# Loading the first kernel tile through two queues, and negating its second half on VectorE

## The chip, the cores and the metric

The kernel runs on one core of a Trainium2 chip. Its time is the device time of one execution in microseconds (us). Each version is executed several times and the median is compared. One execution is also profiled; its trace gives the start, the length and the releaser of each instruction on TensorE (PE, with its weight loads PEld), VectorE (DVE), ScalarE (ACT), GpSimd (POOL) and the DMA queue of SyncE (SP). Trace times are counted from the start of the profiled span.

## The reference

The program computes two independent things and joins their outputs. Part A is a recurrent attention over 64 segments; the change doesn't touch it, but it fills the second two thirds of the time. Part B is a long convolution by way of a transform:

```python
P = jnp.exp(logdA[:, :, None] * l[None, None, :])      # l = 0 .. 2047
K = jnp.einsum('dn,dnl,dn->dl', Cc, P, dB).real        # one kernel per channel d
Kf = rfft2(pad(K))                                     # spectrum of the kernel
Uf = rfft2(pad(u transposed))                          # spectrum of the input
y = irfft2(Uf * Kf)[..., :L] transposed + u * Dskip
```

There are D = 1024 channels, N = 128 states and L = 2048 positions; all inputs are bf16.

## The kernel before

Part B comes first and part A follows. Part B is written in an order set by hand: each engine and each queue carries out its instructions in the order in which the program names them.

**Tables.** The kernel K is built from tables of exponentials and sines, 64 channels at a time, in 16 passes. The loop `for f in range(-1, 17)` (line 1116) walks the words of the list ORDER (line 600). A word names an operation and a slot; a prime means that the word belongs to the pass before (r = f - 1), so the passes overlap. The last iteration, f = 16, has only the primed words of pass 15 left to do. The words that matter here:

- `b0'`, `b1'`: `absolute`, line 1068, an absolute value in place on `nr` (VectorE, 128x1856, four bytes an element).
- `w0'`, `w1'`: `minus`, line 1075, `wn`, minus the sine (VectorE, 128x768 bf16).
- `C0'`, `C1'`: `cosine`, line 1071 (ScalarE), after `absolute`.
- `gi`, `gr`: `products`, lines 1019 and 1020 (VectorE), from the sine or cosine and the exponentials.
- `K0'` to `K3'`: `part`, line 910, small matmuls into `kp` (TensorE), and `x0'` to `x3'`: `part_out`, line 918, which casts `kp` into `KxT` (VectorE).
- After pass 3, 7, 11 and 15 `KxT` holds 256 channels and is written to `Kd` in DRAM by a set of small DMAs (line 925), taken one by one from the list `late`. What is left at the end goes to SP and GpSimd in turn.

**Side work.** Between these words other work is done in small portions: `U` (the input's spectrum, line 866, with sums `us` on VectorE, lines 877 and 878, sums `ux` on GpSimd, lines 882 to 885, and a write to `Ud`, line 886), `M` (transposed matrices, `ms`, line 849, written to `MId` by GpSimd, line 850), and `P` (projections that part A will need, lines 145 and 158, with writes `PVd` and `PKd` on SP).

**The first kernel tile.** At f = 15 the first 512 channels of K have long been in DRAM. `load_k` (line 946) fetches them as one tile `KT` of 128x16x512 bf16 with 31 DMAs (line 954), from rows that are interleaved for the transform. Its argument `qs` is a tuple of queues that take the DMAs in turn; here it holds SP alone. `negate` (line 987) makes `KN`, minus the second half of `KT` (128x4096), with one tensor_scalar: before, on GpSimd (line 990), at the word `m'` of f = 15. In GpSimd's queue it stands behind the Ud write of the previous portion and ahead of the MId write and the ux sums of its own.

**The spectrum of the kernel.** `spectrum(0)` (line 1007), first thing of f = 16, is 64 matmuls on TensorE into the PSUM tiles `pa` and `ptt`; 16 of them read KN. From then on a loop over b = 0 to 15 makes `spectrum(b + 1)`, multiplies with the input's spectrum on VectorE (`pointwise`, lines 1182 to 1193, input `uq` by line 981 on SP), and from b = 4 transforms back (`inverses`, line 1240, with `uu` loaded and written by GpSimd). The later channels of K are loaded at b = 0 by 62 DMAs on GpSimd (line 954 too).

Of the kernel before, what the change touches and what calls it, by code (L numbers as in the profile page):

```python
# [10 lines left out]
BF16 = mybir.dt.bfloat16  # L11
# [595 lines left out]
def part_b(ctx, tc, u, A_re, A_im, B_re, B_im, C_re, C_im, log_dt, Dskip, out_b, ahead, copies, residents, first_state):  # L607
# [5 lines left out]
    DH, DQ = 512, 256  # L613
    v, sc, gp, pe, sy = nc.vector, nc.scalar, nc.gpsimd, nc.tensor, nc.sync
# [331 lines left out]
    def load_k(d0, n_d, qs, KT):  # L946
        dsl = slice(d0, d0 + n_d)

        def rows(r0, n, step=1):
            return Kd[r0:r0 + step * (n - 1) + 1:step, dsl]  # L950
        n_q = [0]

        def get(out, in_):
            qs[n_q[0] % len(qs)].dma_start(out=out, in_=in_)
            n_q[0] += 1
        for r in (0, 2, 1, 3):
            k0 = KT[:, 4 * r, :]
            get(k0[0:64], rows(r, 64, 4))
            get(k0[64:128], rows(256 + (0, 0, 1, 2)[r], 64, 2))
            k1 = KT[:, 4 * r + 1, :]  # L960
            if r == 2:
                get(k1[0:128:2], rows(384, 64, 2))
                get(k1[1:128:2], rows(386, 64, 2))
            else:
                get(k1[:], rows(384 + (0, 0, 0, 1)[r], 128))
            for mc in (2, 3):
                k2 = KT[:, 4 * r + mc, :]
                q0 = 512 + 64 * (mc - 2)
                get(k2[0:128:2], rows(q0, 64))
                if r == 0:  # L970
                    get(k2[1:128:4], rows(q0, 32, 2))
                    get(k2[3:128:4], rows(q0 + 2, 32, 2))
                else:
                    get(k2[1:128:2], rows(q0 + 1, 64))
        return KT

    def load_u(b):
        us = []
        for n_ in range(2):
            t_ = ahead.pool.tile([128, 2, 2, DQ], F32, name="uq", tag="wsl", bufs=4)  # L980
            sy.dma_start(out=t_[:].rearrange("p a c d -> p (a c d)"), in_=Ud[b % 4, b // 4][:, 2 * n_:2 * n_ + 2].rearrange("p a c d -> p (a c d)"))
            us.append(t_)
        return us
# [3 lines left out]
    def negate(KT, eng=None):  # L987
        KN = ahead.pool.tile([128, 8, DH], BF16, name="KN", tag="xTl")
        if eng:
            eng.tensor_scalar(out=KN[:], in0=KT[:, 8:16, :], scalar1=-1.0, scalar2=None, op0=ALU.mult)  # L990
        else:
            for i in range(2):
                sc.activation(out=KN[:, :, DQ * i:DQ * i + DQ], in_=KT[i][:, 8:16, :], func=ACT.Copy, scale=-1.0)
        KNs.append(KN)

    def spectrum(b, s_):
        dq, kc = b // 4, b % 4
        KN = KNs[dq // 2]
        d = slice(DQ * (dq % 2), DQ * (dq % 2) + DQ)
        KT = ks[0][:, :, d] if dq < 2 else ks[dq - 1][:]  # L1000
        for half in range(2):
            for r in range(2):
                for cs in range(2):
                    for i, rr in enumerate((r, r + 2)):
                        for mc in range(4):
                            rhs = KN[:, 4 * (rr - 2) + mc, d] if half == 1 and i == 1 else KT[:, 4 * rr + mc, :]
                            pe.matmul(s_[r][half][:, cs, :], lhsT=MF[:, kc, 4 * rr + mc, cs, :], rhs=rhs,  # L1007
                                      start=(i == 0 and mc == 0), stop=(i == 1 and mc == 3), skip_group_check=True)
# [83 lines left out]
    def run_side(kind, slot):  # L1092
        for g in side_ops[kind]:
            f_ = next(g, g)
            if f_ is not g:
                pending[kind, slot] = f_
                return

    def run_evict(kind, slot, copy):
        f_ = pending.pop((kind, slot), None)  # L1100
        if f_ is not None and f_.__code__.co_argcount:
            f_(copy)
        elif f_ is not None:
            f_()
# [11 lines left out]
    for f in range(-1, 17):  # L1116
        if f == 15:
            for kind, slot in sorted(k for k in pending if k[0] == "P"):
                run_evict(kind, slot, v.tensor_copy)
            while ahead.late:  # L1120
                ahead.late.pop(0)()
            ks = [load_k(0, DH, (sy,), ahead.pool.tile([128, 16, DH], BF16, name="KT", tag="kst"))]
        if f == 16:
            spectra = [load_u(0), load_u(1)]
        for word in ORDER:
            nm, r = word.rstrip("'"), f - word.endswith("'")
            if f == 15 and word == "m'":
                negate(ks[0], gp)
            if f == 16 and word == ORDER[0]:
                s0 = ps_e.tile([128, 2, 512], F32, name="pa", tag="pa")  # L1130
                s1 = [ps_t.tile([128, 512], F32, name="ptt", tag="ptt") for _ in range(2)]
                first = [[s0[:, half, :].rearrange("p (c d) -> p c d", c=2) for half in range(2)],
                         [t_[:].rearrange("p (c d) -> p c d", c=2) for t_ in s1]]
                spectrum(0, first)
            if nm in evict_of:
                run_evict(*evict_of[nm])
            elif nm[0] in side_ops:
                if f >= 0:
                    run_side(nm[0], int(nm[1:] or 0))
            elif nm[0] == "X":  # L1140
                e = int(nm[1])
                if 0 <= r <= 15 - (e == 0) or (r == -1 and e == 0):
                    table_ops[nm[2]](r, e)
            elif 0 <= r <= 15:
                table_ops[nm[:-1]](r, int(nm[-1]))
# [171 lines left out]
def kernel(  # L1317
# [88 lines left out]
    with ExitStack() as ctx_b:  # L1406
        part_b(ctx_b, tc, B_u[0], B_A_re, B_A_im, B_B_re, B_B_im, B_C_re, B_C_im, B_log_dt, B_Dskip, out_b, ahead, copies, residents, first_state)
# [37 lines left out]
```

## Time and profile before

| what | value |
|---|---|
| median of 4 executions | 2399.77 us (2392.59 to 2406.52) |
| profiled execution | 2392.59 us |
| its span | 2390.9 us |
| busy: PE / PEld | 2002.3 / 1179.9 us |
| busy: DVE / ACT / POOL | 1481.6 / 976.9 / 362.1 us |
| mean granted TensorE clock | 0.966 |

The tables end at about 487 us, the loop over b runs to about 700 us, part A fills the rest. The stretch around the end of the tables, by the view of busy time per window:

| window, us | PE busy | DVE busy | POOL busy | granted clock | DMA share |
|---|---|---|---|---|---|
| 436 to 444 | 6.09 | 8.00 | 7.66 | 1.00 | 0.36 |
| 456 to 462 | 5.83 | 4.16 | 2.77 | 1.00 | 0.40 |
| 462 to 477 | 8.10 | 15.00 | 14.68 | 0.77 | 0.46 |
| 477 to 484 | 1.07 | 6.73 | 2.26 | 0.59 | 0.40 |
| 484 to 490 | 5.48 | 3.52 | 2.27 | 0.50 | 0.14 |
| 490 to 540 | 36.73 | 48.87 | 34.22 | 0.88 | 0.87 |
| 540 to 600 | 60.00 | 56.47 | 25.50 | 1.00 | 0.53 |

The granted clock is the share of full speed that TensorE was given; the DMA share is the mean busy share of the core's 16 DMA engines. In a timeline line the columns are the start, the length, the engine, the line of the program, the operation, output<-input, and in brackets the idle time before it with what ended it. "SPq" is the issue of a DMA by SyncE.

### The profile page before, as it was taken

The page shows a single profiled execution, that of the slowest core. Times are in us where ns is not written, and L with a number is a line of the kernel's source. Part 1 is how long each engine was busy: PE and PEld are TensorE (multiplying, and loading weights), DVE is VectorE, ACT ScalarE, POOL GpSimd, SP SyncE. Part 2 cuts the span into 40 slices and gives each one's busy share as a digit, 9 for nine tenths or more (in the row PEclk, how much of TensorE's full clock was granted, in tenths as well). Part 3 has the DMA queues.
Part 4 walks back from the last instruction along what each step waited for, and adds up shares of the span by engine and source line. Part 5 has one row for each costly group of instructions (what it writes and reads, how often), then busy time and mean ns, then how long its engine had stood idle before and what let it go on. Part 6 is the DMA issues. An engine that isn't in the chain of part 4 may idle for free.

```text
span 2390.9 us, 78400 instructions
## 1 busy us (share of the span) xinstructions
PE 2002.3 (84%) x33773; PEld 1179.9 (49%) x33798; DVE 1481.6 (62%) x3159; ACT 976.9 (41%) x1599; POOL 362.1 (15%) x609
## 2 busy tenths in 40 slices
PE   1699999769997888888888888888888888888889
PEld 1366665558883444444444444444444444444444
DVE  9599999999973555545455454554545545454540
ACT  6699999713342323323232232323323233332321
POOL 2245354564121000000000000000000000000020
PEclk6799999889998999999999999999999999999999
DMA  6786985575479999999999999999999999999992
GB/s 160 185 242 201 246 224 147 168 235 183 139 265 377 384 376 388 375 371 385 368 387 384 369 374 374 380 365 372 380 385 373 372 380 384 385 384 388 386 384 74
DMA packets 380384, 759.08 MB, mean 317 GB/s; under 512 B 121704, under 2 KB 213960, under 8 KB 377988
## 3 DMA queue, kind: packets, MB, share of 16 engines
q1 hardware_dynamic: 365316, 710.87, 82.6%
q0 software_dynamic: 14720, 43.20, 5.4%
q8 instruction: 264, 4.33, 0.7%
q14 instruction: 84, 0.69, 0.1%
HBM read 699.16 MB, written 67.88 MB: 321 GB/s over the span
## 4 chain that ended last, share of the span: by engine, by line
DMA 35%; PE 32%; DVE 15%; issue 8%; ACT 6%; SPq 1%; POOL 1%; ACTq 0%; DVEq 0%; POOLq 0%
DMA wst<-WD_k 14%; PE acc L349 14%; DMA wst<-WD_o 12%; PE pp L448 3%; DMA wst<-WD_v 3%; DVE nr L1068 2%; PE pe L571 2%; PE pro L158 2%; PE tr L360 2%; DMA out_dram<-uu 2%; PE ups L866 2%; DMA wst<-WD_q 2%; PE pa L1037 2%; DVE piece L282 1%; DMA KT<-Kd 1%
## 5 line engine op out<-in xcount | busy, mean ns | idle before, releaser
L349 PEld LDWEIGHTS <-hT 128*32 128x32 bf16 x12352 | 326.9, 97 | 454.5 <-issue 230.7
L349 PE MATMUL acc<-wst,hT 128*32 128x512 bf16 x3072 | 312.8, 391 | 145.7 <-DMA wst<-WD_q 51.0
L349 PE MATMUL acc<-W,hT 128*32 128x512 bf16 x5120 | 400.9, 384 | 0.0
L355 ACT CAST ev<-acc 128x512 bf16<-128x512 f32 x384 | 225.1, 586 | 399.6 <-PE acc L349 394.6
L448 PEld LDWEIGHTS <-oT 128*32 128x32 bf16 x8192 | 204.1, 97 | 122.6 <-issue 96.4
L282 DVE TENSOR_SCALAR piece<-keep 128x256 int32<-128x256 int32 (+1 forms) x640 | 192.4, 363 | 60.2 <-PE pp L448 31.9
L387 DVE TENSOR_REDUCE mx<-sc 128x8 f32<-128x320 f32 x128 | 62.4, 487 | 232.4 <-PE sc L380 232.3
L448 PE MATMUL pp<-W_o,oT 128*32 128x256 bf16 x4096 | 184.0, 277 | 5.5 <-DMA W_o<-in_A_Wo_dram 5.3
L361 DVE COPY KT<-tr 128x512 bf16<-128x512 bf16 x64 | 27.2, 425 | 259.4 <-PE tr L360 259.4
L448 PE MATMUL pp<-wst,oT 128*32 128x256 bf16 x2560 | 129.0, 278 | 43.2 <-DMA wst<-WD_o 34.0
L349 PE MATMUL acc<-MF,hT 128*32 128x512 bf16 x2048 | 158.5, 383 | 0.0
L368 POOL COPY KT<-pk 128x128 bf16<-128x128 bf16 x128 | 37.9, 296 | 783.5 <-PE sc L380 433.6
L361 ACT COPY QT<-tr 128x512 bf16<-128x512 bf16 x128 | 75.0, 586 | 178.7 <-PE tr L360 177.8
L435 ACT CAST oT<-pv 128x512 bf16<-128x512 f32 x128 | 75.1, 586 | 171.7 <-PE pv L421 170.1
L321 POOL COPY hT<-xt 128x192 bf16<-128x192 bf16 x63 | 22.0, 350 | 737.3 <-DMA xt<-XTd 446.5
L1007 PEld LDWEIGHTS <-MF 128*128 128x128 bf16 x1024 | 103.7, 102 | 36.0 <-issue 15.7
L158 PE MATMUL pro<-xTl,wsl 128*128 128x512 bf16 x493 | 116.3, 381 | 6.0 <-ACT xTl L102 5.2
L389 ACT ACTIVATE sc<-sc 128x320 f32<-128x320 f32 x128 | 54.0, 422 | 153.9 <-DVE sc L388 145.6
L360 PEld LDWEIGHTS <-ev 128*128 128x128 bf16 x1024 | 58.2, 98 | 97.3 <-issue 66.7
L1007 PE MATMUL hps<-KT,MF 128*128 128x256 bf16 x720 | 94.0, 283 | 13.8 <-DVE x L1183 10.7
L1240 PE MATMUL yp<-Bt,MI 128*128 128x256 bf16 x680 | 102.8, 273 | 0.8 <-ACT yb L1256 0.8
L360 PE MATMUL tr<-a_ident,ev 128*128 128x128 bf16 x1024 | 102.2, 223 | 0.0
(315 smaller groups left out, 3808.1 us busy)
## 6 DMA issues: line engine op xcount, KB each, us to landing
wst<-WD_o SPq DMA_DIRECT2D x320, 512.0 KB
wst<-WD_k SPq DMA_DIRECT2D x256, 512.0 KB
wst<-WD_q SPq DMA_DIRECT2D x256, 512.0 KB
wst<-WD_v SPq DMA_DIRECT2D x256, 512.0 KB
Ud<-ux POOLq DMA_DIRECT2D x16, 1024.0 KB, 5.7
uq<-Ud SPq DMA_DIRECT2D x32, 512.0 KB
pk<-PKd SPq DMA_DIRECT2D x64, 192.0 KB
wsl<-in_A_Wk_dram SPq DMA_DIRECT2D x16, 512.0 KB
```

The source lines that it names most:

```text
L158: nc.tensor.matmul(a[:], lhsT=w[:, kc, 128 * j:128 * j + 128], rhs=xTl[:, kc, :, :].rearrange("p s k -> p (s k)"), start=(kc == 0), stop=( ...
L282: nc.vector.tensor_scalar(out=out.bitcast(I32), in0=in_.bitcast(I32), scalar1=0, scalar2=None, op0=ALU.bitwise_or)
L349: nc.tensor.matmul(a[32 * g:32 * g + 32, o_:o_ + rhs.shape[1]], lhsT=hT[:, kc, :], rhs=rhs, start=(kc == 0), stop=(kc == KC - 1), tile_pos ...
L355: nc.scalar.copy(out=q[:], in_=a[:])
L360: nc.tensor.transpose(out=p[:, i, hl, :, :].rearrange("p a b -> p (a b)"), in_=q[:, 128 * hl:128 * hl + 128], identity=ident[:])
L361: eng(out=dst, in_=p[:, i, :, :, :])
L387: nc.vector.tensor_reduce(out=mx[:], in_=sc, axis=AX.X, op=ALU.max)
L389: nc.scalar.activation(out=sc, in_=sc, func=ACT.Exp, scale=scale)
L435: nc.scalar.copy(out=o[:], in_=p[:].rearrange("p a (g q) -> p a g q", g=4))
L448: nc.tensor.matmul(po[32 * qt:32 * qt + 32, :], lhsT=oT[:, h % 4, (h % 16) // 4, :], rhs=columns(w, 1024 * hh + 256 * qt, 256)[0][1], star ...
L1007: pe.matmul(s_[r][half][:, cs, :], lhsT=MF[:, kc, 4 * rr + mc, cs, :], rhs=rhs, start=(i == 0 and mc == 0), stop=(i == 1 and mc == 3), ski ...
L1240: pe.matmul(yp[:, b, :], lhsT=m_[:, b, cs, kc, :], rhs=Bt[:, kc, j, half, c_, :], start=(kc == 0 and cs == 0 and half == 0), stop=(kc == 3 ...
```

## The change

`KT` is loaded by SP and GpSimd in turn: DMAs 1, 3, 5 and so on go to SP (16), DMAs 2, 4, 6 and so on to GpSimd (15). `negate` moves from GpSimd, at the word `m'` of f = 15, to VectorE, at the start of f = 16, directly before `spectrum(0)` is issued. In VectorE's queue that places it behind the last cast `KxT` of `x3'` (f = 15) and ahead of `b0'` of f = 16. The data and their layout stay the same.

```diff
-            ks = [load_k(0, DH, (sy,), ahead.pool.tile([128, 16, DH], BF16, name="KT", tag="kst"))]
+            ks = [load_k(0, DH, (sy, gp), ahead.pool.tile([128, 16, DH], BF16, name="KT", tag="kst"))]
         if f == 16:
             spectra = [load_u(0), load_u(1)]
         for word in ORDER:
             nm, r = word.rstrip("'"), f - word.endswith("'")
-            if f == 15 and word == "m'":
-                negate(ks[0], gp)
             if f == 16 and word == ORDER[0]:
                 s0 = ps_e.tile([128, 2, 512], F32, name="pa", tag="pa")
                 s1 = [ps_t.tile([128, 512], F32, name="ptt", tag="ptt") for _ in range(2)]
                 first = [[s0[:, half, :].rearrange("p (c d) -> p c d", c=2) for half in range(2)],
                          [t_[:].rearrange("p (c d) -> p c d", c=2) for t_ in s1]]
+                negate(ks[0], v)
                 spectrum(0, first)
```

## The prediction

> **What bounds the kernel now.** I read the chain that ended last first, in order of time, because the change touches some 40 us of a 2390.9 us span and only a place on the chain can pay. Columns: start, length, what.
>
> ```profile
> 462.27 8.51 DVE nr L1068
> 470.79 5.58 DVE wn L1075
> 483.79 3.19 PE kp L910 x73
> 497.69 5.05 DMA PKd<-PVd
> 502.93 4.91 POOL KT L954 x9
> ```
>
> Two VectorE instructions of the last table pass are the longest pieces of this stretch, and the path then runs through kp, the Kd writes, the PKd copies and GpSimd's later KT loads into the pointwise phase. Next I read the timeline of VectorE, one table pass earlier and in the last pass (start us, length, what):
>
> ```profile
> 438.64 1.58 DVE L1068 TENSOR_SCALAR nr<-nr 128x1856 int32<-128x1856 int32 x1
> 440.15 0.88 DVE L1075 TENSOR_SCALAR wn<-sn 128x768 bf16<-128x768 bf16 x1
> 440.95 1.65 DVE L1068 TENSOR_SCALAR nr<-nr 128x1856 int32<-128x1856 int32 x1
> ...
> 462.24 8.54 DVE L1068 TENSOR_SCALAR nr<-nr 128x1856 int32<-128x1856 int32 x1
> 470.71 5.66 DVE L1075 TENSOR_SCALAR wn<-sn 128x768 bf16<-128x768 bf16 x1
> 476.29 1.12 DVE L1068 TENSOR_SCALAR nr<-nr 128x1856 int32<-128x1856 int32 x1
> 477.32 1.11 DVE L1019 TENSOR_TENSOR gi<-E,sn 128x1824 bf16<-128x1824 bf16 x1
> ```
>
> The same three instructions take 3.88 us from start to start of the next work in one pass (438.64 to 442.52, where the next row begins) and 15.08 us in the other (462.24 to 477.32). Their shapes are equal. GpSimd's timeline says what differs:
>
> ```profile
> 421.03 2.23 POOL L896 DMA_DIRECT2D pt<-PB  x4
> ...
> 438.52 4.67 POOL L885 TENSOR_TENSOR ux<-us 128x256 f32<-128x256 f32 x4
> 443.48 0.57 POOL L886 DMA_DIRECT2D Ud<-ux  x1 [0.30 <-POOL ux L885]
> 459.24 10.57 POOL L990 TENSOR_SCALAR KN<-KT 128x4096 bf16<-128x4096 bf16 x1 [15.18 <-DMA PVd<-vst]
> 469.77 1.13 POOL L850 DMA_DIRECT2D MId<-ms  x1
> 470.93 1.28 POOL L882 TENSOR_TENSOR ux<-us 128x512 f32<-128x512 f32 x1
> 472.16 1.27 POOL L883 TENSOR_TENSOR ux<-us 128x512 f32<-128x512 f32 x1
> 473.38 2.76 POOL L885 TENSOR_TENSOR ux<-us 128x256 f32<-128x256 f32 x4
> ```
>
> KN runs on GpSimd until 469.81, and L1068, begun at 462.24, ends at 470.78: about its own 1.12 us after KN. The wn behind it, 0.34 us when alone (the shortest of its 32), ends at 476.37, 0.23 us after the last ux. So these VectorE forms do not run while GpSimd works on SBUF. The negation on GpSimd costs VectorE its own length, and it also pushes ux (ready at 459.56, as the us row before it ends then) onto wn.
>
> SP's timeline carries the loads:
>
> ```profile
> 435.94 21.25 SPq L954 DMA_DIRECT2D KT<-Kd  x31
> ```
>
> **The change, part by part.** VectorE is on the path all the way from 462.24 to 477.32: no idle stands before any of these rows. I rebuild this stretch.
>
> *GpSimd loses KN, gains 15 load issues.* They stand where the table pass begins, behind the Ud write, so they start at 444.05 (443.48 + 0.57). The first of them waits for old Kd writes and for the kst tile's last DMA (issued 429.62), all past. Nearest rows: L896, four in 2.23 us, 0.56 each, at this same phase of an earlier pass; L954 itself, later, fifteen from 502.93 to 511.25, 0.55 each with landing waits. So 15 x 0.55 = 8.3 us, done at 452.4; landing, by KT's own DMAs, 3.3 to 7.2 us: 455.7 to 459.6. They are gone from the queue before MId, whose ms comes at 458.0. So MId and ux go back to their usual phase: ux's first row at 459.65, its L885 rows from 462.13, as in the pass before (first ux 436.05, L885 438.52).
>
> *The rule that speaks against this part* is in the Trainium skill, SBUF — State Buffer, section SBUF: two separate sides: descriptors of a DMA issued from GpSimd cannot be written while VectorE is in a two-port mode, and an issue of some 620 ns then took 3100. At that price the 15 issues take 46.5 us, end at 490.6, land at 495.8. The trace has rows for issues beside VectorE's work in this phase, 0.56, and the slowest Ud issue, in the last pass, is 1.08. In 444 to 452 VectorE runs products with two inputs, conversions, and only one wn (448.95, 0.36 us). I take the row: the rule costs 0.4 us here, hidden by 2.6 us or more of slack, if only wn can hold an issue up.
>
> *SP loses 15 of 31 issues.* At 21.25/31 = 0.69 each, SP is through at about 447 instead of 457.2. What follows (PVd, Kd, uq) moves earlier, but the next thing that matters on SP, the Kd writes of the last table, waits for KxT at 487 in any case. Worth nothing by itself.
>
> *VectorE gains KN*, queued behind the last KxT of the pass and ahead of L1068. It waits for KT's second half, landed by 459.6, so it can start at 462.24; queued behind it are both L1068, wn, and all products of the last pass. Length: no such row. Fitting fixed + per-element time to 1.116 us for 1856 four-byte elements and 0.343 for 768 two-byte ones at half the time each gives 0.141 us + n x 0.263 ns for bf16: 4096 elements take 1.22 us. Ends: below, 1.2; above, at L1068's time per element, 2.29. I take 1.22, since wn has the same operation and type.
>
> *Contention left.* ux's four L885 rows run from 462.13. In the pass before, each VectorE row waited for one of them (1.58, 0.88, 1.65 instead of 1.12, 0.34, 1.12). Now KN takes the first wait: KN 0.5 + 1.15 = 1.65, then 1.51, 0.80 and 1.57 (start to start in the pass before) make 5.5 us. **Saved: 15.08 - 5.5 = 9.5 us.**
>
> *A second rule to weigh*: the same page, section Who interferes with whom, says whoever issues first holds the shared pair for one whole instruction. By it KN loses at most one L885, 0.69 us. The row at 470.71 disagrees: wn waited through six GpSimd instructions. If KN does as wn did, it waits 2.76 us, but nothing is left for the others to wait for: 2.76 + 1.15 + 1.04 + 0.27 + 1.04 = 6.3, saved 8.8. Without any contention 3.5, saved 11.6. I take 9.5, the pattern of the pass before, because the phase is the same.
>
> *TensorE* waits 5.43 us for KN at 464.4 now. After: KN is ready at about 463.9. Its 32 remaining matmuls, at the 0.11 us of the first 16, end at 468, before gr (470.9). The 5.43 us are not added: they lay beside VectorE's stall. What is late next: VectorE's products, then kp. ACT's two cosines follow L1068 by 1.84 us and come before their products.
>
> *Does the shift reach the end?* After KxT come Kd writes, PKd copies, KT loads (502.93) and pointwise steps. All are behind KxT in their queues, so they move together. From 540 to 660 TensorE is busy 60.0 of each 60 us at clock 1.00 and DMA at 0.53 and 0.43: fixed work, its start moves. From 700 on the weights' stream holds DMA at 0.96; its slots come free as the phase ends, so it moves too.
>
> **The sum.** Profiled execution 2392.59 (span 2390.9) - 9.5 = 2383.1. It was the fastest of four; the same 9.5 off the median 2399.77 gives **2390**, which I forecast.
>
> **Rivals.**
>
> *More is gained.* No contention (11.6), and TensorE stays warm for kp: the clock is 0.59 and 0.50 in 477 to 490, where kp holds VectorE up for 2.0 us. Three quarters of kp took 1.7 us at 435, all of it 3.2 us here; at the faster pace (1.7 x 4/3 = 2.3) about 0.9 us go. Together 12.5: 2387. Against: TensorE still idles before gi ends, and each pass shows the contention.
>
> *Nothing arrives.* The gain ends in a wait on the DMAs that does not move, such as uu at 550, for which VectorE waits 2.08 us behind GpSimd's KT loads. Then 2400. Against: these loads are themselves behind KxT.
>
> *Slower: the loads on GpSimd land late.* KN is at the head of VectorE's queue, and everything waits for it. The gain is gone once the last load lands after 462.24 + 9.5 = 471.7: with 5.2 us of landing, when an issue takes over (471.7 - 5.2 - 444.05)/15 = 1.5 us. At the slowest row, 1.08, landing is at 465.5 and 6.2 us of gain are left. At the rule's 3.1 us, KN starts 33.6 us late: 24 us slower, 2424.
>
> *The change not doing what it says* is out: queue order has KN on VectorE and 15 loads on GpSimd.
>
> **How the numbers follow.** Forecast 0.60, more 0.25, nothing 0.08, slower 0.07. A measurement of this kernel tells about 0.5% from no change, 12 us. The forecast lies below that; the four runs spread over 14 us, so a third of its cases may measure above it, and about two thirds of the richer case: 0.19 + 0.16 = 0.35 faster. Slower: 0.06 from its rival, 0.02 from noise. Same: the rest, 0.57. The range: the four runs, less 9.5, are 2383 to 2397; unknown costs (8.4 with the long KN, 12.5 in the richer case) widen it down to 2380, noise of a median on another day and the case of no gain up to 2401; I take 2379 to 2401. The slower case is left out.
>
> **What would show it.** KN on VectorE at about 462.3, 1.2 to 1.8 us; L1068 and wn of the last pass at some 1.6 and 0.9; 15 KT issues of 0.55 on GpSimd from 444; no idle before TensorE's KN matmuls; the first pointwise row (L1182, now 488.22) near 478.7, and the uu wait and the end moved as much. It is wrong if KN waits for DMA past 464, if ux runs elsewhere than at 459.6 to 466, or if L1182 moves and the end does not.

## The result and the profile after

The changed kernel takes 2388.07 us (median of 40 executions, 2378.34 to 2399.77) against 2399.71 us (61 executions, 2390.62 to 2413.08) for the kernel before. The ratio of the mean times is 0.9956 with a 95% interval of 0.9946 to 0.9965: 10.6 us less, between 8.4 and 13 (the two medians lie 11.6 us apart). The profiled execution took 2383.52 us with a span of 2381.8, 9.1 us less than the span before. Its mean granted clock is 0.981, where the profile before has 0.966; the difference lies mostly ahead of the place of the change (0.93 before, 1.00 now, up to 440 us), and at the end of it VectorE comes to the stretch in question only 0.76 us earlier. Below line 1127 the changed program has one line less, so line 1182 of before is line 1181 here.

VectorE's timeline, around the end of the tables, in the changed kernel:

```profile
461.48 1.73 DVE L990 TENSOR_SCALAR KN<-KT 128x4096 bf16<-128x4096 bf16 x1
463.13 1.64 DVE L1068 TENSOR_SCALAR nr<-nr 128x1856 int32<-128x1856 int32 x1
464.70 0.88 DVE L1075 TENSOR_SCALAR wn<-sn 128x768 bf16<-128x768 bf16 x1
465.50 1.65 DVE L1068 TENSOR_SCALAR nr<-nr 128x1856 int32<-128x1856 int32 x1
467.08 1.11 DVE L1019 TENSOR_TENSOR gi<-E,sn 128x1824 bf16<-128x1824 bf16 x1
...
477.97 1.23 DVE L1181 TENSOR_TENSOR x<-pa,osb__7239 128x1024 f32<-128x1024 f32 x1 [0.78 <-ACT osb__7239 L1175]
...
504.72 1.23 DVE L1186 TENSOR_TENSOR y<-uq,x 128x1024 f32<-128x1024 f32 x1 [0.71 <-DMA uq<-Ud]
```

L1068 and wn are back at the lengths of the pass before (1.64, 0.88, 1.65 instead of 8.54, 5.66, 1.12). From the start of KN to the start of gi it is 5.60 us; from the start of the first L1068 to that of gi it was 15.08: 9.48 us less. The first pointwise row starts 10.25 us earlier than before (488.22); 0.76 of this was there already at 461.48, ahead of the stretch. The last row shows a small new wait, for the third uq load, that the kernel before did not have.

GpSimd's timeline of the same execution:

```profile
444.39 3.80 POOL L954 DMA_DIRECT2D KT<-Kd  x7 [0.29 <-DMA KT<-Kd]
448.69 1.12 POOL L954 DMA_DIRECT2D KT<-Kd  x2 [0.50 <-DMA Ud<-ux]
450.27 3.26 POOL L954 DMA_DIRECT2D KT<-Kd  x6 [0.46 <-DMA KT<-Kd]
457.58 0.57 POOL L850 DMA_DIRECT2D MId<-ms  x1 [4.06 <-DVE ms L849]
458.94 1.27 POOL L882 TENSOR_TENSOR ux<-us 128x512 f32<-128x512 f32 x1 [0.78 <-DVE us L877]
460.18 1.27 POOL L883 TENSOR_TENSOR ux<-us 128x512 f32<-128x512 f32 x1
461.41 4.76 POOL L885 TENSOR_TENSOR ux<-us 128x256 f32<-128x256 f32 x4
...
487.85 11.51 POOL L954 DMA_DIRECT2D KT<-Kd  x21 [1.86 <-DMA Kd<-KxT]
```

The 15 issues take 0.54 us each and are through at 453.5; MId and ux follow ms and us at once again, as in the pass before. The L885 rows and VectorE's rows take turns: the former stretch from 2.76 to 4.76 us, the latter by half a microsecond each. The later KT loads start at 487.85, 15.1 us earlier than before (502.93), which is more than the shift.

Where does the gain go in the end? TensorE's timeline shows its last waits ahead of the long transform phase, in the kernel before

```profile
526.25 5.67 PE L1007 MATMUL hps<-KT,MF 128*128 128x256 bf16 x36 [6.52 <-DVE x L1183]
```

and in the changed one:

```profile
516.81 5.92 PE L1007 MATMUL hps<-KT,MF 128*128 128x256 bf16 x36 [7.32 <-DVE x L1182]
```

From this point TensorE shows no further wait up to 671.6 us in the kernel before and 662.4 in the changed one; its work there is fixed, 13.97 us for each b. The point lies 9.44 us earlier (0.76 of this is again the head start), the next wait 9.2 and the end of the program 9.1. The chain of waits of the changed kernel passes GpSimd's later loads only on its way to the third uq load, and from 516.81 on it names TensorE's run, where the chain before kept to the loads up to 546 (start, length, what):

```profile
487.85 4.41 POOL KT L954 x8
...
494.46 2.83 DMA KT<-Kd
497.35 7.28 DMA uq<-Ud
504.72 1.24 DVE y L1186
...
516.81 15.96 PE hps L1007 x128
```

### The profile page after: what moved, and what is told of

It reads as the page before. It is cut to its first block, busy times and chain, and to the rows that moved or that the text cites. A ratio compares the mean times of both kernels' runs of the same rounds, so it can differ in the third digit from the quotient of the medians.

```text
span 2381.8 us, 78406 instructions
## 1 busy us (share of the span) xinstructions
PE 1996.9 (84%) x33773; PEld 1177.3 (49%) x33798; DVE 1470.9 (62%) x3160; ACT 977.1 (41%) x1599; POOL 362.9 (15%) x623
## 4 chain that ended last, share of the span: by engine, by line
PE 38%; DMA 31%; DVE 18%; ACT 6%; issue 4%; SPq 1%; POOL 1%; DVEq 0%; ACTq 0%; POOLq 0%
DMA wst<-WD_k 15%; PE acc L349 12%; DMA wst<-WD_o 10%; PE yp L1239 4%; PE hps L1007 4%; PE pp L448 3%; DMA wst<-WD_v 3%; PE pe L571 2%; PE pro L158 2%; DVE nr L1068 2%; DMA wst<-WD_q 2%; PE ups L866 2%; PE tr L360 2%; PE pa L1037 2%; DVE piece L282 1%
## 5 line engine op out<-in xcount | busy, mean ns | idle before, releaser
L1007 PE MATMUL hps<-KT,MF 128*128 128x256 bf16 x720 | 93.0, 281 | 15.5 <-DVE x L1182 12.4
```

## The experiments

All ratios are to the kernel before on the same chip. An interval is 2.3 to 5.4 us to each side, so small effects are read from the traces. As a ruler for them I use the distance from the point where VectorE is done with x3' of f = 15 (the start of the row behind it, or the end of the cast where that row has to wait) to the start of TensorE's unbroken run:

| kernel | VectorE free | unbroken run | distance | ratio (95%) |
|---|---|---|---|---|
| before | 462.24 | 526.25 | 64.0 | 1 |
| changed | 461.48 | 516.81 | 55.3 | 0.9956 (0.9946 to 0.9965) |
| negation only | 462.56 | 517.08 | 54.5 | 0.9948 (0.9926 to 0.9971) |
| second queue only | 462.79 | 524.73 | 61.9 | 0.9993 (0.9978 to 1.0008) |
| TensorE doesn't wait | 461.35 | 528.52 | 67.2 | 0.9999 (0.9985 to 1.0012) |
| unread GpSimd work | 462.14 | 523.25 | 61.1 | 0.9987 (0.9972 to 1.0002) |
| GpSimd alone loads | 461.68 | 525.03 | 63.4 | 0.9983 (0.9967 to 0.9999) |
| early KN, two queues | 462.44 | 515.77 | 53.3 | 0.9956 (0.9938 to 0.9974) |
| early KN, one queue | 461.73 | 515.12 | 53.4 | 0.9954 (0.9933 to 0.9976) |
| MId write on SP | 461.12 | 525.74 | 64.6 | 0.9992 (0.9978 to 1.0006) |

The distances are of one execution each; those of the kernels with KN on GpSimd depend on when the last part of KT landed in it.

### One half of the change each

Negation only:

```diff
-ks = [load_k(0, DH, (sy, gp), ...)]
+ks = [load_k(0, DH, (sy,), ...)]
```

> SP loads all 31 parts of KT as before; only the negation moves to VectorE. Theory (the gain is KN leaving GpSimd, the second queue is worth nothing): KT is in by 459.2 as before, KN runs on VectorE from 461.5 to 462.3 with 1.7 us, L1068 and wn at 1.6 and 0.9, first pointwise row near 478; ratio to before 0.996. Rival (the second queue is needed): KN waits for DMA to 464 or later and the ratio is 0.998 or more.

Measured: 2387.64 us, 0.9948. VectorE's timeline (first fence) and GpSimd's (second):

```profile
462.56 1.74 DVE L990 TENSOR_SCALAR KN<-KT 128x4096 bf16<-128x4096 bf16 x1
464.23 1.65 DVE L1068 TENSOR_SCALAR nr<-nr 128x1856 int32<-128x1856 int32 x1
```

```profile
493.33 7.71 POOL L954 DMA_DIRECT2D KT<-Kd  x14 [4.20 <-DMA PKd<-PVd]
```

KN has no idle time before it: with SP alone its data are there in time. The negation carries the whole gain, as far as the intervals tell.

Second queue only:

```diff
-ks = [load_k(0, DH, (sy,), ...)]      # kernel before, negate(ks[0], gp) stays
+ks = [load_k(0, DH, (sy, gp), ...)]
```

> KT by two queues, KN still on GpSimd. Theory: the last load lands near 457, so KN starts on GpSimd about 2 us earlier than 459.24, still 10.6 us long; L1068 then waits for it until about 468 and wn waits for ux; at most 2 us are gained, ratio 0.999 to 1.000. Rival (the second queue carries the gain): ratio 0.997 or less.

Measured: 2397.98 us, 0.9993. VectorE, then GpSimd:

```profile
462.79 6.15 DVE L1068 TENSOR_SCALAR nr<-nr 128x1856 int32<-128x1856 int32 x1
468.86 5.66 DVE L1075 TENSOR_SCALAR wn<-sn 128x768 bf16<-128x768 bf16 x1
```

```profile
457.39 10.56 POOL L990 TENSOR_SCALAR KN<-KT 128x4096 bf16<-128x4096 bf16 x1 [2.70 <-PE ptt L1031]
```

KN starts 1.85 us earlier than before and VectorE comes 0.55 later, so the stretch to gi (475.48) is 12.7 us, 2.4 less than before, where 2 at most were expected. The time can't be told from that of before, though the interval leaves room for these 2 us.

### What made VectorE wait

First the rival that TensorE's 5.43 us wait for KN was the loss. In the kernel before it is this row:

```profile
469.85 1.01 PE L1007 MATMUL pa<-KN,MF 128*128 128x256 bf16 x4 [5.43 <-POOL KN L990]
```

This variant leaves out the minus sign in the first block, so that spectrum(0) needs no KN:

```diff
-rhs = KN[...] if half == 1 and i == 1 else KT[...]
+rhs = KN[...] if half == 1 and i == 1 and b > 0 else KT[...]
```

> Before, with one change: spectrum(0) reads KT where it would read KN, so that TensorE does not wait for KN (its values for the first block differ). KN is still made on GpSimd at the same place. Theory (VectorE's stall is the path, TensorE's 5.4 us lie beside it): L1068 still about 8.5 us, wn about 5.7, ratio 1.000. Rival (TensorE's wait for KN was what the change removed): ratio 0.998, 5 us less.

Measured: 2398.32 us, 0.9999. VectorE's timeline:

```profile
461.35 1.13 DVE L1068 TENSOR_SCALAR nr<-nr 128x1856 int32<-128x1856 int32 x1
462.39 10.72 DVE L1075 TENSOR_SCALAR wn<-sn 128x768 bf16<-128x768 bf16 x1
473.03 6.67 DVE L1068 TENSOR_SCALAR nr<-nr 128x1856 int32<-128x1856 int32 x1
479.61 1.11 DVE L1019 TENSOR_TENSOR gi<-E,sn 128x1824 bf16<-128x1824 bf16 x1
```

The expected lengths were missed: in this execution, the slowest of its 22, KN began on GpSimd only at 461.82, and the first L1068 got in ahead of it. So wn waited for KN and the second L1068 for ux, and the stretch was 18.3 us, 3.2 longer than before. TensorE's matmuls of spectrum(0) ran through without a wait. From gi to the unbroken run it is 48.9 us in both kernels (479.61 to 528.52, before 477.32 to 526.25): the distance is longer by just what VectorE lost more. TensorE's wait cost nothing; VectorE's did.

Then GpSimd's work without any data that someone needs, added to the changed kernel:

```diff
+if f == 15 and word == "m'":
+    for i in range(2):
+        unread = ahead.pool.tile([128, 4, DH], BF16, name="unread", tag="wsl", bufs=4)
+        gp.tensor_scalar(out=unread[:], in0=ks[0][:, 8 + 4 * i:12 + 4 * i, :], scalar1=-1.0, ...)
```

> As changed, plus two GpSimd negations of 128x2048 into tiles that nothing reads, where KN stood on GpSimd: no engine waits for their data. Theory (GpSimd's work itself holds VectorE's rows up): GpSimd runs them from about 457 to 468; KN on VectorE stretches to 6 us or more, wn or L1068 behind it wait for ux; most of the gain is gone, ratio 0.999 to 1.002. Rival (the gain came from the order of data, not from GpSimd's work): the ratio stays at 0.996. If a VectorE row waits for one GpSimd instruction only, KN takes about 2.5 us if it comes late in the first of the two, up to 6.5 if early; if it waits for both, to 468.

Measured: 2395.04 us, 0.9987. VectorE, then GpSimd:

```profile
462.14 4.63 DVE L990 TENSOR_SCALAR KN<-KT 128x4096 bf16<-128x4096 bf16 x1
466.69 6.42 DVE L1068 TENSOR_SCALAR nr<-nr 128x1856 int32<-128x1856 int32 x1
473.03 0.35 DVE L1075 TENSOR_SCALAR wn<-sn 128x768 bf16<-128x768 bf16 x1
...
474.34 1.11 DVE L1019 TENSOR_TENSOR gi<-E,sn 128x1824 bf16<-128x1824 bf16 x1
```

```profile
454.93 10.76 POOL L1130 TENSOR_SCALAR unread<-KT 128x2048 bf16<-128x2048 bf16 x2
465.63 1.26 POOL L850 DMA_DIRECT2D MId<-ms  x1
466.92 1.27 POOL L882 TENSOR_TENSOR ux<-us 128x512 f32<-128x512 f32 x1
...
469.37 2.76 POOL L885 TENSOR_TENSOR ux<-us 128x256 f32<-128x256 f32 x4
```

Nobody waits for these tiles, and yet 6.6 of the 9.5 us in the stretch are lost again (12.2 us instead of 5.6; the interval reaches from 0.5 us above the time of before to 6.7 us below it, and lies wholly above that of the changed kernel). So it is GpSimd's occupation that holds these VectorE rows up, not the order of the data. KN waited for the second of the two rows only, which began ahead of it, and took 4.63 us where 6 or more were expected, as GpSimd's rows ran two us earlier than assumed; L1068 behind it waited for all of ux.

### The slower rival priced

The price of 3.1 us an issue is the one that the prediction took from the Trainium skill.

```diff
-ks = [load_k(0, DH, (sy, gp), ...)]
+ks = [load_k(0, DH, (gp,), ...)]
```

> As changed, but GpSimd alone issues all 31 loads of KT. It prices the slower rival of the forecast. By the changed kernel's trace (0.54 us an issue, 15 in 9.1 us with the waits for landing) the 31 are issued from 444.4 to about 465, the last lands near 469; KN on VectorE waits for it and starts 7 to 8 us later than in the changed kernel; MId and ux are late too, but then run while VectorE stands still. Most of the gain goes: ratio 0.998 to 1.000. By the rule of starved descriptors (3.1 us an issue) it would be 96 us of issues and a ratio above 1.02.

Measured: 2394.50 us, 0.9983. VectorE, then GpSimd:

```profile
468.25 4.99 DVE L990 TENSOR_SCALAR KN<-KT 128x4096 bf16<-128x4096 bf16 x1 [6.57 <-DMA KT<-Kd]
```

```profile
465.84 0.55 POOL L954 DMA_DIRECT2D KT<-Kd  x1 [0.15 <-DMA KT<-Kd]
466.39 0.55 POOL L850 DMA_DIRECT2D MId<-ms  x1
466.95 1.27 POOL L882 TENSOR_TENSOR ux<-us 128x512 f32<-128x512 f32 x1
468.18 1.26 POOL L883 TENSOR_TENSOR ux<-us 128x512 f32<-128x512 f32 x1
469.40 2.76 POOL L885 TENSOR_TENSOR ux<-us 128x256 f32<-128x256 f32 x4
```

The rival's mechanism exists: KN waits 6.57 us at the head of VectorE's queue, and then for the rest of ux. But an issue still takes 0.55 us beside the VectorE rows that run here, so even all 31 loads on GpSimd eat only some 6.5 of the 10.6 us; the 15 of the change are far from it. A price of 3.1 us an issue is out for this stretch.

### A better place for KN

The second half of KT loaded first, and KN put ahead of ms, where VectorE idles; with two queues and with SP alone:

```diff
-for r in (0, 2, 1, 3):
+for r in order_r:                       # (2, 3, 0, 1) for this tile
...
+if f == 15 and word == "m'":
+    negate(ks[0], v)
...
-                negate(ks[0], v)        # at the start of f = 16
```

> As changed, but the second half of KT is loaded first and KN stands on VectorE ahead of ms, where VectorE idles for 1.3 us. Theory: KN has landed data by 453, takes 1.2 us in the idle gap and meets no GpSimd work; L1068, wn, L1068 follow the last KxT with 1.6, 0.9, 1.65 us; 1.7 us less than the changed kernel, ratio 0.995. If the loads land after 455, VectorE waits for them and the gain is smaller.

> The same, with SP alone loading KT: 15 parts of the second half are issued by about 447, landed by about 452, before KN's place at 455. Theory: KN in the gap as with two queues; and the later loads of KT on GpSimd, about 4 us later than with two queues, do not hold up the third uq load (0.8 us in the changed kernel): some 2.5 us less than the changed kernel, ratio 0.9945. Rival (the second queue is needed to have KT early): KN waits beyond 456.5 and ms, MId and ux move back with it.

Measured: 2389.35 us, 0.9956, and 2386.25 us, 0.9954. VectorE with one queue:

```profile
455.40 1.22 DVE L990 TENSOR_SCALAR KN<-KT 128x4096 bf16<-128x4096 bf16 x1
...
461.73 1.58 DVE L1068 TENSOR_SCALAR nr<-nr 128x1856 int32<-128x1856 int32 x1
...
465.60 1.64 DVE L1019 TENSOR_TENSOR gi<-E,sn 128x1824 bf16<-128x1824 bf16 x1
```

KN fits into the gap at 1.22 us and meets nobody. The distance is 2 us shorter than in the changed kernel: the 1.7 us expected in the stretch come, 0.5 of them go back, because the fourth ux row now meets gi (1.64 instead of 1.11), and the 0.71 us of the wait for the third uq load are gone in both versions. In time both versions can't be told from the changed kernel, nor from each other: no version here is shown to beat it.

### One row or a whole series

```diff
-gp.dma_start(out=MId[c], in_=ms[:])
+(sy if c == 15 else gp).dma_start(out=MId[c], in_=ms[:])    # kernel before
```

> Before, with one change: SP, not GpSimd, issues the last write to MId, which stood between KN and ux on GpSimd. It asks why wn waited through all six ux rows there, when in other passes a VectorE row waits for one GpSimd row only. If a row that comes up while GpSimd issues a DMA is passed over by the rows behind it, wn now waits for one ux row at most (1.6 us, not 5.7), the stretch from L1068 to gi falls from 15.1 to 12 to 13, ratio 0.999. If the DMA issue has no part in it, wn still takes about 5.7 and the ratio is 1.000.

Measured: 2395.89 us, 0.9992, which tells neither from 1.000 nor from 0.999. VectorE, then GpSimd:

```profile
461.12 10.12 DVE L1068 TENSOR_SCALAR nr<-nr 128x1856 int32<-128x1856 int32 x1
471.16 1.42 DVE L1075 TENSOR_SCALAR wn<-sn 128x768 bf16<-128x768 bf16 x1
472.50 2.19 DVE L1068 TENSOR_SCALAR nr<-nr 128x1856 int32<-128x1856 int32 x1
474.61 1.65 DVE L1019 TENSOR_TENSOR gi<-E,sn 128x1824 bf16<-128x1824 bf16 x1
```

```profile
459.69 10.57 POOL L990 TENSOR_SCALAR KN<-KT 128x4096 bf16<-128x4096 bf16 x1 [15.93 <-DMA PVd<-vst]
470.25 2.12 POOL L882 TENSOR_TENSOR ux<-us 128x512 f32<-128x512 f32 x1
472.32 1.38 POOL L883 TENSOR_TENSOR ux<-us 128x512 f32<-128x512 f32 x1
```

Without the DMA issue between KN and ux the two engines take turns from row to row, and wn waits for one ux row. From the end of KN to gi it is 4.35 us (470.26 to 474.61) against 7.5 before (469.81 to 477.32). The whole stretch is 13.5 us, above the 12 to 13 expected, and the four products behind it meet the remaining ux rows and lose some 2.1 us more, so that the distance is no shorter than before (64.6 to 64.0). And the DMA issue can't be the only cause: where GpSimd alone loads KT, KN came up at 468.25, 1.3 us after the last DMA issue had ended, and still waited through five ux rows. What decides between one row and a series stays open.

## Why the prediction was right

Its forecast, 9.5 us less and a median of 2390 us, holds: 10.6 us less by the ratio of the means, 9.1 by the two profiles, and 2388.07 us. That the two profiles agree so closely with 9.5 is partly luck, since executions of either kernel spread over more than 20 us. Its figure for what a measurement can tell, 12 us, was too coarse: with this many executions the interval reaches about 2.3 us to each side, so that 10.6 us stand clear of no change. Step by step:

- **The stretch.** Forecast 5.5 us with KN at 1.65, L1068 and wn at 1.6 and 0.9; measured 5.60 with 1.73, 1.64, 0.88, 1.65. Saved 9.48 for 9.5. That GpSimd's work was the cause is shown by the unread work; that TensorE's wait was not, by the kernel in which it is gone.
- **KN's length.** The fit gave 1.22 us; alone in its gap KN takes 1.22 us. The other end, 2.29, is out.
- **Contention.** The choice of the pass before as a pattern was right, and so here is the rule that the first to issue holds the shared pair for one whole instruction (the Trainium skill, SBUF — State Buffer, Who interferes with whom): each row, KN to the second L1068, came out about 0.5 us longer than alone, as if it waited for one L885. Read as a bound of one GpSimd instruction the rule fails elsewhere: in five kernels, before included, a row waited through five or six GpSimd rows.
- **The loads.** 15 issues of 0.54 us, for 0.55; KN had no wait for DMA. The 3.1 us of the Trainium skill (SBUF — State Buffer, SBUF: two separate sides) do not appear: one wn of 0.39 us lay in that window. The page gives them for a DMA beside one VectorE copy, so 15 times 3.1 was a reach in any case. Beside the negation the second queue shows no gain (0.9956 with it, 0.9948 without).
- **TensorE.** The forecast end of spectrum(0), 468, is 466.8 in the trace; it waits for no KN, and this gains nothing by itself.
- **More gained.** It did not come: kp still took 3.19 us and held VectorE up for 1.97 (0.71 and three times 0.42), at a granted clock of 0.53 in 474 to 480, where before it was 0.50 in 484 to 490; and contention stayed.
- **Where the shift goes.** Right in the result, wrong in the way. The prediction led the path through GpSimd's later KT loads and feared the uu wait at 550. But TensorE had been running without a wait from 526.25 already, so from there on these loads set nothing: with the negation only they start 5.5 us later than in the changed kernel (493.33), and the time is not longer. Nor did the uu wait move with the end, as forecast: of the 2.08 us before, the negation only has 1.08 left (at 541.12) and the changed kernel none, and neither shows in the time. What counts is VectorE's row that releases TensorE at b = 3. The chain shows one way back from the end, not the only one, and not that TensorE ran without a gap beside it.
- **A term not seen.** With two queues the later KT loads start 15.1 us earlier, not 9.5, and the third uq load arrives 0.71 us late for VectorE. The distance grows by 0.8 us against the negation alone (55.3 to 54.5). Of the five kernels in which GpSimd takes loads of the first tile three have such a wait (0.71, second queue only 0.26, GpSimd alone 1.16) and two have none; of the five with SP alone none has it. The second queue thus seems to cost a little at times where it was put at nothing; no interval here can show that in the time, and why two kernels escape was not tried.

## What to carry to other kernels

Before work is given to an idle engine, look at what runs beside it and whether that grows longer: 10.57 us of work on an idle GpSimd cost VectorE 9.48 us here, although GpSimd was busy for only 362 of 2391 us. The sign in a profile is a row whose length jumps while its shape stays the same; compare it with the same row of another pass and look at who was at work until it ended. And read the path's end from the engine that stops waiting: once TensorE ran without a gap here, waits of others beside that run cost nothing, though the chain named them.

## What the runs showed of the hardware

- VectorE's products with two inputs are also held up by GpSimd's sums: gi took 1.64 us instead of 1.11 when an ux row ran beside it (early KN), and up to 1.65 and 1.09 for 1.11 and 0.56 where the MId write is on SP.
- A GpSimd DMA issue is held up by these VectorE rows too: MId's took 1.13 us in the kernel before and with the second queue only, and 1.26 with the unread work, while L1068 or KN ran, and 0.55 to 0.62 in the other kernels that issue it from GpSimd.
- The same negation takes 10.57 us on GpSimd and 1.22 us on VectorE.
- When the later KT loads start went with how many loads of the first tile SP issues. In the five kernels where SP issues all 31 (before, negation only, TensorE doesn't wait, early KN with one queue, MId write on SP) GpSimd waits for a PKd copy and starts them 14.5 to 15.5 us after the last KxT; in the five where it issues 16 or none they start after 10.7 to 10.9 us. Why was not tried.
